# mLSTM cell and leaky-ReLU feed-forward on one core: half of a weight's loads on a second queue, and another hand order for the first chunk

## The chip, the cores and the metric

One NeuronCore of a Trainium2 chip runs the whole program. Its engines work side by side, each through its own list of instructions in order: TensorE (PE; its weight loads are shown as PEld), VectorE (DVE), ScalarE (ACT), GpSimd (POOL) and SyncE (SP). Transfers between the chip's main memory (HBM) and the on-chip memory (SBUF, 128 partitions) are started by an instruction on SP, ACT or POOL and carried by 16 DMA engines. Matmul results go to PSUM.

The metric is the device time of one execution in microseconds (us), the median of several.

## The reference, cut to what matters

```python
# q, k, v, o_gate: (4, 8, 768, 40) float32;  i_gate, f_gate: (4, 8, 768) float32
for t in range(S):                               # mLSTM cell, per batch and head
    m_new  = max(f[t] + m, i[t])
    f_stab = exp(f[t] + m - m_new);  i_stab = exp(i[t] - m_new);  m = m_new
    C = f_stab * C + i_stab * outer(v[t], k[t])  # 40 x 40 state
    n = f_stab * n + i_stab * k[t]
    y[t] = sigmoid(o[t]) * (C @ q[t]) / max(|n . q[t]|, 1)
x = y as (3072 tokens, 320)
h = x @ w_in                                     # 320 x 2048
out = max(0.01 * h, h) @ w_out                   # 2048 x 320
```

The two weights arrive as 64-bit floats (they were scaled by a 64-bit number), so a w_in of 320 x 2048 is 5.24 MB in HBM, as is w_out.

## The kernel before, in words

**Chunks and steps.** The 768 positions are cut into 6 chunks c of 128. A step s = 4c + b is chunk c of batch b, with its 8 heads. `NL = 4` sets of k, q, v and state tiles (`kn`, `qn`, `S0` to `S3`) go round, and `NR = 2` tiles `rb` for the later loads. The feed-forward of chunk c - 1 (`ff_units`, L777) runs on PE between the cell units of chunk c (`cell_units`, L842); chunk 0 has no feed-forward to lie beside it and is written out by hand in `first_chunk` (L887), with the first two feed-forward units `ffs[0]` and `ffs[1]` in it.

**Chunk 0.** `gates(c)` (L289) makes the stabilised gates with two scans and small operations on DVE, into one buffer each; `gates_exp` adds exponentials on ACT; `gates_T` (L341) transposes them through PE and copies them to `gT` on DVE. `spread_mask` and `spread_first` (L442, L453) build the decay matrix in PSUM with PE: a causal mask (`ident_b`, a bf16 identity, times `cmask`) and then the gate rows. `prep_exp` (L474) takes its exponential on ACT into `w`. `u_transpose` (L565) transposes k and q of a step on PE and copies them out (`kqT`), `u_scores` (L576) multiplies them and DVE weights the scores with `w` (L587), `u_values` (L660) multiplies by v and makes the denominators, `gate` (L668) applies the output gate (its second multiply on POOL, or on DVE where that is named), `u_x` (L756) transposes the result into `xT` through five copies, `u_state` (L650) makes the state at the chunk's end from `vu` (`prep_vu`, L483, on POOL) and copies it into the S tiles. `prepare_step` (L160) and `prepare_tiles` (L152) set constants on POOL. The steps 0 to 3 share one set of four PSUM banks for all this (`psc`) and another four for mask and feed-forward (`psf`).

**Chunk 1 and later.** `u_split` (L547) transposes k and q of a step of chunk 1 in halves (line L557), `split_qs` transposes the decayed q (L543), `u_parts` (L621) makes scores and state additions (L637, L642), `u_plain` (L679) the values (L688). `ahead(s)` prepares a step on ACT and POOL, `feed(s)` issues its k, v and decay loads.

**Feed-forward.** The first half of a unit multiplies x by w_in into `ph` (L783), ACT applies the leaky ReLU into `acts` (L791), the parts multiply `acts` by w_out into `po` (L818). w_in is held as two stacks of 64 partitions: the lower half `r = 0` and the upper half `r = 1`, in quarters n of 512 columns. For chunk 0 the units are 16 halves of 20 matmuls, then 16 parts; two of the halves lie in `first_chunk`, so the loop over i (L996) begins with the third, and the parts begin at i = 14.

**Weights.** `load_weights(n)` (L199) loads a raw 64-bit block: n = 0 to 3 are the quarters of w_in, each as four transfers on SP (L227), two for each half of the partitions; n = 4 to 11 are the eight blocks of w_out (L233), issued on ACT's queue at the units i named in `fetch` (L983). A w_out block from the third on lands in a buffer which an earlier block's conversion must have left. `narrow_weights(n)` (L235) turns a raw block into float32, in six instructions of ACT and DVE, as a generator: each `run(w, k)` issues the next k of them. For n < 2 the form is ACT (L248), DVE (L250, L254, L258), ACT (L260), DVE (L262); for the others ACT (L265, L267), DVE (L269), ACT (L273), DVE (L275, L279). In the loop the generator `now` runs through blocks 2 to 11, a few instructions at each i (L998).

**What sets the order.** PE, DVE, ACT and POOL do their work in the order of the code (`manual_schedule`, L971). SP's order is chosen by a scheduler from the code's order and its own estimates. Each transfer takes one of eight completion semaphores in turn, whichever of SP and ACT issues it, and waits for the transfer that had the same one before; so at most eight are under way on these two queues, and a queue can wait for a transfer of the other.

Of the kernel before, what the change touches and what calls it, by code (L numbers as in the profile page):

```python
# [21 lines left out]
def kernel(  # L22
# [81 lines left out]
    zeros = consts.tile([P, 1], F32, name="zeros")  # L104
    nc.vector.memset(zeros[:], 0.0)
    first = consts.tile([P, 1], F32, name="first")
    nc.scalar.activation(first[:], zeros[:], AF.Exp)


    ident_b = consts.tile([P, P], BF16, name="ident_b")  # L110
# [3 lines left out]
        cmask[:], cmask[:], compare_op=ALU.is_ge, fill=-1e30,  # L114
        base=0, pattern=[[1, P]], channel_multiplier=-1,
    )
    nc.vector.tensor_copy(ident_b[:], ident[:])
    cm2 = i0[:, :SL]


# [12 lines left out]
    for n in range(NL):  # L133
        nc.vector.memset(kn[:, n, :, D:], 0.0)
        nc.vector.memset(qn[:, n, :, D:], 0.0)
        nc.gpsimd.memset(S_t[n][:, 1, :, D:], 2.0)
        nc.gpsimd.memset(S_t[n][SL:, 0], 0.0)

    def mixed(s):

# [39 lines left out]
        at = (2 * slot + e) * P  # L180
        return w_in[DP * r : DP * (r + 1), n, at : at + P]

    def run_of(r, at):

        ks = SLOTS[r][at:]
        return ks[0], next((i for i in range(1, len(ks)) if ks[i] != ks[i - 1] + 2), len(ks))

    HW = 2 * Dm
    wide = moe_w_in.dtype == U64
    raws = {}  # L190
# [5 lines left out]
        ks = SLOTS[r][at:]  # L196
        return ks[0], next((i for i in range(1, len(ks)) if ks[i] != ks[i - 1] + 2), len(ks))

    def load_weights(n):  # L199

        m = n - QN
        if n < QN:
            dst = w_in[:, n, :]
        else:
            dst = w_out[:, 2 * m : 2 * m + 2, :].rearrange("p a d -> p (a d)")
        to = dst
        if wide:
            if n < 2:
                at = NF * GT - 2 * WC * (n + 1)
                raw = acts_l[:, at : at + 2 * WC].bitcast(U64)  # L210
            elif n < QN:
                raw = raw_t[:, WC * (n - 2) : WC * (n - 1)]
            elif m < 2:
                raw = w_out[:].rearrange("p f d -> p (f d)")[:, (2 + m) * WC : (3 + m) * WC].bitcast(U64)
            else:
                at = (4, 0, 1, 2, 3, 4)[m - 2] * HW
                raw = raw_t[:, at : at + HW]
            raws[n] = (raw, dst)
            to = raw
        if n < QN:  # L220
            src = moe_w_in[:, n * QC : (n + 1) * QC].rearrange("(k p) (r c) -> r p k c", p=DP, r=2)
            by_slot = to.rearrange("p (k c) -> p k c", k=KC)
            for r in range(2):
                at = 0
                while at < KC:
                    k0, many = run_of(r, at)
                    nc.sync.dma_start(  # L227
                        by_slot[DP * r : DP * (r + 1), at : at + many, :], src[r, :, k0 : k0 + 2 * many - 1 : 2, :],
                    )
                    at += many  # L230
        else:
            rows = moe_w_out[2 * m * P : 2 * (m + 1) * P, :]
            nc.scalar.dma_start(to.rearrange("p (a d) -> p a d", d=Dm), rows.rearrange("(a p) d -> p a d", p=P))  # L233

    def narrow_weights(n):  # L235

        if not wide:
            return  # L240
        raw, dst = raws.pop(n)
        words = raw.bitcast(U32).rearrange("p (c two) -> p c two", two=2)
        lo, hi = words[:, :, 0], words[:, :, 1]
        d = dst.bitcast(U32)
        words = raw.bitcast(U32)[:, : dst.shape[-1]]
        ends = words.bitcast(U16).rearrange("p (c two) -> p c two", two=2)
        if n < 2:
            nc.scalar.activation(dst, hi.bitcast(F32), AF.Abs)  # L248
            yield
            nc.vector.tensor_scalar(  # L250
                dst, dst, scalar1=2.0**-15, scalar2=122879.9921875, op0=ALU.max, op1=ALU.min,
            )
            yield
            nc.vector.tensor_scalar(  # L254
                d, d, scalar1=0x07FFFFFF, scalar2=3, op0=ALU.bitwise_and, op1=ALU.logical_shift_left,
            )
            yield
            nc.vector.scalar_tensor_tensor(d, in0=hi, scalar=0xC0000000, in1=d, op0=ALU.bitwise_and, op1=ALU.bitwise_or)  # L258
            yield
            nc.scalar.activation(words, lo, AF.Copy, scale=2.0**-29)  # L260
            yield
            nc.vector.tensor_tensor(d, d, words, op=ALU.add)  # L262
            yield
            return
        nc.scalar.activation(dst, hi.bitcast(F32), AF.Abs, scale=2.0**16)  # L265
        yield
        nc.scalar.activation(ends[:, :, 0], lo, AF.Copy, scale=2.0**-29)  # L267
        yield
        nc.vector.tensor_scalar(  # L269
            dst, dst, scalar1=2.0, scalar2=122879.9921875 * 2.0**16, op0=ALU.max, op1=ALU.min,  # L270
        )
        yield
        nc.scalar.activation(ends[:, :, 1].bitcast(F16), hi.bitcast(F32), AF.Copy, scale=2.0**-126)  # L273
        yield
        nc.vector.tensor_scalar(  # L275
            d, d, scalar1=0x1FFFFFFF, scalar2=3, op0=ALU.bitwise_and, op1=ALU.logical_shift_left,
        )
        yield
        nc.vector.tensor_tensor(d, d, words, op=ALU.add)  # L279
        yield  # L280
# [100 lines left out]
    def load_o(s):  # L381
        c, b = divmod(s, B)
        at = NF * GT - 4 * WC - (s + 1) * Dm
        st[s]["o"] = acts_l[:, at : at + Dm]
        nc.sync.dma_start(
            st[s]["o"].rearrange("p (h d) -> p h d", d=D), o_gate[b, :, ts(c, P), :].rearrange("h p d -> p h d"),
        )
# [86 lines left out]
    def prep_exp(s):  # L474

        c, b = divmod(s, B)
        w = st[s]["w"]
        for h in range(H):
            bh = b * H + h
            of = st[s]["ab"][h % RG][:, h // RG, :] if c == 0 else w[:, h, :]  # L480
            yield nc.scalar.activation(w[:, h, :], of, AF.Exp, bias=gT[c][:, 0, bh : bh + 1], scale=1.0)  # L481
# [168 lines left out]
    def u_state(s):  # L650
        state(s)
        state_copy(s)
# [186 lines left out]
    def u_gates(c):  # L839
        gates_T(c, bus.pop(c)[0])  # L840
# [15 lines left out]
    def run(steps, n=None):  # L856

        for _ in range(H if n is None else n):
            next(steps, None)
# [27 lines left out]
    def first_chunk():  # L887

        tensor_copy = nc.vector.tensor_copy
        for part in (slice(0, 2), slice(2, 3)):  # L890
            load(0, part)
            load(1, part)
        load_o(0)
        load_o(1)
        load_weights(0)
        load(2)
        load(3)
        load_o(2)
        load_o(3)
        load_weights(1)  # L900
        load_weights(2)
        warm(5)
        spread_mask(0)
        warm(2)
        gates(0)
        gates_exp(0)
        load_fi(2)
        bu, a, _ = bus[0]
        spread_first(a, 0)
        gates_T(0, bu)  # L910
        run(prep_exp(0))
        u_transpose(0, tensor_copy)
        prep_vu(0)
        gates(1)
        u_transpose(1, tensor_copy)
        u_scores(0)
        run(prep_exp(1))
        prepare_tiles()
        prep_vu(1)
        u_scores(1)  # L920
        u_state(0)
        gates_exp(1)
        prep_o(0)
        prep_o(1)
        u_values(0)
        gate(0)
        spread_mask(2)
        spread_first(a, 2)
        run(prep_exp(2))
        u_state(1)  # L930
        u_x(0, tensor_copy)
        u_values(1)
        gate(1, nc.vector)
        w = narrow_weights(0)
        run(w, 3)
        run(prep_exp(3))
        u_gates(1)
        u_x(1)
        prep_vu(2)
        u_transpose(2, tensor_copy)  # L940
        run(w, 2)
        u_scores(2)
        run(w)
        u_transpose(3)
        prep_o(2)
        prep_o(3)
        ffs = ff_units(0)
        ffs[0]()
        prep_vu(3)
        prepare_step(0)  # L950
        prepare_step(1)
        u_values(2)
        gate(2, nc.vector)
        u_scores(3)
        u_x(2)
        ffs[1]()
        u_state(2)
        w = narrow_weights(1)
        run(w, 2)
        u_values(3)  # L960
        gate(3, nc.vector)
        run(w, 2)
        u_x(3)
        u_state(3)
        run(w)
        prepare_step(2)
        prepare_step(3)
        return ffs

    E = mybir.EngineType  # L970
    with tc.manual_schedule(engines={E.PE, E.DVE, E.Activation, E.Pool}):  # L971
        ffs = first_chunk()
        for s in (B, B + 1):
            feed(s)
            for i in range(1, 3):
                load_late(s, i)
        load_weights(3)
        for s in (B + 2, B + 3):
            feed(s)


        ffs = ffs[2:]
        fetch = {4: (0, 1, 2), 6: (3, 4), 10: (5, 6), 15: (7,)}  # L983
        place = (2, 5, 7, 10, 12, 15, 16, 18, 21, 22, 24, 26, 28)
        late = {}
        masks = {0: (2, 3), 12: (4, 5)}
# [2 lines left out]
        for c in range(1, NB + 1):  # L989
# [5 lines left out]
            waiting = []  # L995
            for i in range(n_ff):  # L996
                if c == 1:
                    run(now, (2, 2, 2, 0, 2, 2, 2)[i] if i < 7 else 2 if i < 13 else 3)  # L998
                    for n in fetch.get(i, ()):
                        load_weights(QN + n)  # L1000
                    if i == 0:
                        prep_mask(B)
                        ahead(B)
                        load_fi(3)
# [70 lines left out]
```

## Time and profile before

| | |
|---|---|
| median of 3 runs (lowest to highest) | 544.42 us (544.06 to 544.57) |
| profiled execution | 544.73 us |
| its span, first to last instruction | 542.9 us |
| mean granted PE clock | 0.965 |
| busy: PE, PEld | 520.1 us (96%), 341.3 us (63%) |
| busy: DVE, ACT, POOL | 206.8 us (38%), 184.3 us (34%), 107.3 us (20%) |
| moved by DMA | 59.12 MB, mean 109 GB/s |

Two groups of matmuls hold most of PE's time: `ph` (L783), 1120 of them, 221.0 us, and `po` (L818), 768, 211.1 us. The rest of the profile is read by stretches of time, since the first part of the span differs from all that follows. A row of the time line has start, length, engine, line, operation, tiles and count, and in brackets the idle time before it with what ended that. In the table by stretches an engine's figure is its busy time in that stretch; the clock is the share of full speed that PE was granted; the DMA share is the mean busy share of the 16 DMA engines as recorded, which can exceed 1.

### The profile page before, as it was taken

What the parts mean: (1) busy time and instruction counts of PE and PEld (TensorE: products, weight loads), DVE (VectorE), ACT (ScalarE), POOL (GpSimd) and SP (SyncE); (2) the same over time, 40 slices, a digit from 0 to 9 for tenths busy, and PEclk for the clock granted to TensorE, in tenths of its full rate; (3) what the DMA queues carried; (4) which work ended last, traced back from release to release, by engine and by line L of the source; (5) the groups of instructions that cost most, each with busy time, mean ns of one, the idle gap of its engine ahead of it and who ended that gap; (6) DMA issues with size and microseconds to landing.
All of it is one profiled execution on the core that took longest, in us unless ns stands there. A gap on an engine that the chain in (4) does not pass through costs nothing.

```text
span 542.9 us, 11240 instructions
## 1 busy us (share of the span) xinstructions
PE 520.1 (96%) x4495; PEld 341.3 (63%) x4495; DVE 206.8 (38%) x396; ACT 184.3 (34%) x470; POOL 107.3 (20%) x142
## 2 busy tenths in 40 slices
PE   7877797999999999999999999999999999999997
PEld 6666687977755467755467755567655577644675
DVE  3674632546803826304728124538025521000000
ACT  3363855879652511212503022522013410022100
POOL 4132304323400503102404003303012100000000
PEclk9758798999999999999999999999999999999999
DMA  9998969954623553566642666554651123000000
GB/s 123 157 208 128 167 129 244 227 128 94 139 78 70 124 132 82 146 133 136 149 124 69 146 126 145 147 126 105 147 130 37 38 62 85 24 1 0 13 12 24
DMA packets 164899, 59.12 MB, mean 109 GB/s; under 512 B 128432, under 2 KB 155632, under 8 KB 164848
## 3 DMA queue, kind: packets, MB, share of 16 engines
q1 hardware_dynamic: 162288, 53.04, 47.1%
q10 hardware_dynamic: 2560, 5.37, 3.2%
q8 instruction: 35, 0.57, 0.5%
q14 instruction: 16, 0.13, 0.1%
HBM read 51.68 MB, written 6.70 MB: 108 GB/s over the span
## 4 chain that ended last, share of the span: by engine, by line
PE 87%; DMA 4%; DVE 4%; SPq 2%; ACT 1%; issue 1%; ACTq 0%; DVEq 0%
PE po L818 39%; PE ph L783 37%; PE pT L718 3%; PE sd L637 3%; DMA rb<-in_k_dram 1%; PE pa L664 1%; DMA S<-in_v_dram 1%; PE sd L642 1%; PE ab L460 1%; PE ab L448 1%; DVE kqT L574 1%; PE sc L583 1%; PE hN L688 1%; DMA a_dr<-a 1%; SPq L430 1%
## 5 line engine op out<-in xcount | busy, mean ns | idle before, releaser
L783 PE MATMUL ph<-xT,w_in 64*128 64x512 f32 (+1 forms) x1120 | 221.0, 548 | 7.0 <-ACT acts L791 6.2
L818 PE MATMUL po<-w_out,acts 128*128 128x320 f32 x768 | 211.1, 434 | 0.0
L818 PEld LDWEIGHTS po<-w_out,acts 128*128 128x128 f32 x768 | 144.4, 190 | 62.6 <-issue 3.8
L783 PEld LDWEIGHTS ph<-xT,w_in 64*128 64x128 f32 x1120 | 114.0, 196 | 101.1 <-issue 88.3
L791 ACT ACTIVATE acts<-ph 128x512 f32<-128x512 f32 (+1 forms) x112 | 53.9, 533 | 149.8 <-PE ph L783 146.1
L647 DVE TENSOR_TENSOR qn<-w,sd 64x512 f32<-64x512 f32 x40 | 27.4, 684 | 119.3 <-PE sd L642 64.0
L615 POOL TENSOR_TENSOR S<-S,f 40x336 f32<-40x336 f32 x36 | 29.7, 824 | 136.3 <-PE pT L718 75.5
L472 POOL TENSOR_TENSOR w<-w,i 128x512 f32<-128x512 f32 x20 | 28.0, 1406 | 94.7 <-DMA w<-a_dr 72.6
L481 ACT ACTIVATE w<-w,gT 128x64 f32<-128x64 f32 x160 | 41.3, 338 | 4.7 <-POOL w L472 4.7
L826 ACT COPY y<-po 128x320 f32<-128x320 f32 x12 | 5.1, 425 | 83.7 <-PE po L818 83.7
L826 ACT COPY hn<-po 128x320 f32<-128x320 f32 x12 | 5.1, 426 | 76.9 <-PE po L818 76.9
L534 DVE TENSOR_TENSOR qn<-kqT,ea 64x512 f32<-64x512 f32 x32 | 26.9, 839 | 0.9
L725 DVE STREAM_TRANSPOSE hb<-pT 128x512 f32<-128x512 f32 x16 | 11.4, 715 | 39.1 <-PE pT L718 38.9
L732 POOL TENSOR_TENSOR xb<-xb,den 128x320 f32<-128x320 f32 x16 | 11.6, 727 | 66.6 <-DVE xb L729 66.6
L637 PEld LDWEIGHTS sd<-kqT 40*64 40x64 f32 x640 | 19.9, 135 | 6.1 <-issue 6.1
L637 PE MATMUL sd<-kqT 40*64 40x64 f32 x640 | 21.6, 220 | 0.0
L736 DVE STREAM_TRANSPOSE x<-xb 128x512 f32<-128x512 f32 x16 | 18.1, 1129 | 7.7 <-POOL xb L732 7.7
L528 DVE STREAM_TRANSPOSE kqT<-rb 128x512 f32<-128x512 f32 x32 | 20.5, 679 | 0.0
L642 PE MATMUL sd<-S,vu 64*40 64x42 f32 x576 | 20.0, 214 | 0.4 <-POOL vu L501 0.4
L642 PEld LDWEIGHTS sd<-S,vu 64*40 64x40 f32 x576 | 18.6, 111 | 0.5 <-POOL vu L501 0.5
L619 DVE TENSOR_TENSOR S<-S,sd 40x336 f32<-40x336 f32 x36 | 18.1, 503 | 1.0
L718 PEld LDWEIGHTS pT<-qn,S 128*64 128x64 f32 x512 | 15.6, 138 | 3.6 <-issue 3.5
(135 smaller groups left out, 357.2 us busy)
## 6 DMA issues: line engine op xcount, KB each, us to landing
w<-a_dr SPq DMA_DIRECT2D x40, 128.0 KB
rb<-in_k_dram SPq DMA_DIRECT2D x64, 80.0 KB
rb<-in_q_dram SPq DMA_DIRECT2D x64, 80.0 KB
rb<-in_o_gate_dram SPq DMA_DIRECT2D x64, 80.0 KB
ea<-a_dr SPq DMA_DIRECT2D x32, 128.0 KB
kn<-in_k_dram SPq DMA_DIRECT2D x24, 160.0 KB
raw<-in_moe_w_out_dram ACTq DMA_DIRECT2D x6, 640.0 KB
S<-in_v_dram SPq DMA_DIRECT2D x80, 40.0 KB
```

What stands on the lines that cost most here:

```text
L472: nc.gpsimd.tensor_tensor(w, w, cm2.unsqueeze(1).to_broadcast([P, H, SL]), op=ALU.add)
L481: yield nc.scalar.activation(w[:, h, :], of, AF.Exp, bias=gT[c][:, 0, bh : bh + 1], scale=1.0)
L528: nc.vector.transpose(d["kqT"][:, i].rearrange("p (h t n) -> p h n t", n=TS, t=QW), raw_blocks(s, i, QW).rearrange("p (h n) d -> p h n d", ...
L534: nc.vector.tensor_tensor(mixed(s)[rows, 1 - r], d["kqT"][rows, 1].rearrange("p (h t) -> p h t", t=SL), d["ea"][rows], op=ALU.mult,)
L615: nc.gpsimd.tensor_tensor(new, old, g, op=ALU.mult)
L637: nc.tensor.matmul(bank[1 - u][toks, h, :], lhsT=kqT[rows, 0, ts(h, SL)], rhs=kqT[rows, 1, ts(h, SL)], start=True, stop=True,)
L642: nc.tensor.matmul(dC[u][:, h].rearrange("p k d -> p (k d)"), lhsT=d["ku"][toks, h], rhs=S_v[s % NL][toks, u, h, :, :V1], start=True, stop ...
L647: nc.vector.tensor_tensor(mixed(s)[toks, u], w[toks], bank[1 - u][toks], op=ALU.mult)
L718: nc.tensor.matmul(pT[DP * r : DP * (r + 1), j * P + u * SL : j * P + (u + 1) * SL], lhsT=S[:, u, h, :], rhs=m[:, u, h, :], start=True, st ...
L783: nc.tensor.matmul(ph[r][:, cols], lhsT=w_row(r, slot, j), rhs=xT[DP * r : DP * (r + 1), slot, cols], start=(slot == 0), stop=(slot == KC ...
L791: nc.scalar.activation(acts[:, f, cols], ph[r][:, cols], AF.Prelu, alpha=0.01)
L818: nc.tensor.matmul(po[n][:], lhsT=acts[:, f, ts(n, P)], rhs=w_out[:, f, :], start=(f == 0), stop=(f == NF - 1),)
```

## The change

- `load_weights` gets an argument `halves`. The lower half of a w_in quarter is loaded on SP, the upper half on POOL's own queue. In chunk 0 the two are called in different places; the fourth quarter has both in one call, but each still goes to its queue.
- The eight blocks of w_out are issued on SP instead of ACT: three ahead of the loop, five at the units 4, 8 and 15.
- The second quarter of w_in is converted in the form with three ACT steps (`n < 1` for `n < 2`).
- In chunk 0: the first exponential (which loads ACT's table), the bf16 identity and the setting of the S tiles move into `first_chunk`, behind the first POOL load; on DVE the identity now stands ahead of the first gate scans. `gates(1)` stands before the copies of the transposes. `u_state`, `u_x(0)`, `u_gates(1)`, `prepare_tiles` and the conversions get other places, and `gate(1)`'s second multiply goes from DVE to POOL.
- In the loop the generator `now` issues 2 instructions at each i below 10, 3 below 14 and then 4.
- A function that stood twice is there once, and a `return` stands twice; neither changes what is done.

```diff
-    nc.scalar.activation(first[:], zeros[:], AF.Exp)
-    nc.vector.tensor_copy(ident_b[:], ident[:])
-        nc.gpsimd.memset(S_t[n][:, 1, :, D:], 2.0)
-        nc.gpsimd.memset(S_t[n][SL:, 0], 0.0)
...
-    def load_weights(n):
+    def load_weights(n, halves=(0, 1)):
...
-            for r in range(2):
+            for r in halves:
...
-                    nc.sync.dma_start(
+                    (nc.gpsimd if r else nc.sync).dma_start(
...
-            nc.scalar.dma_start(to.rearrange("p (a d) -> p a d", d=Dm), rows.rearrange("(a p) d -> p a d", p=P))
+            nc.sync.dma_start(to.rearrange("p (a d) -> p a d", d=Dm), rows.rearrange("(a p) d -> p a d", p=P))
...
-        if n < 2:
+        if n < 1:
...
     def first_chunk():
         tensor_copy = nc.vector.tensor_copy
+        load_weights(0, (1,))
+        for n in range(NL):
+            nc.gpsimd.memset(S_t[n][:, 1, :, D:], 2.0)
+            nc.gpsimd.memset(S_t[n][SL:, 0], 0.0)
+        nc.scalar.activation(first[:], zeros[:], AF.Exp)
+        nc.vector.tensor_copy(ident_b[:], ident[:])
         for part in (slice(0, 2), slice(2, 3)):
             load(0, part)
             load(1, part)
+        load_weights(0, (0,))
         load_o(0)
         load_o(1)
-        load_weights(0)
...
-        load_weights(1)
-        load_weights(2)
+        load_weights(1, (0,))
+        load_weights(2, (0,))
...
         gates_T(0, bu)
+        gates(1)
         run(prep_exp(0))
         u_transpose(0, tensor_copy)
         prep_vu(0)
-        gates(1)
         u_transpose(1, tensor_copy)
         u_scores(0)
         run(prep_exp(1))
-        prepare_tiles()
         prep_vu(1)
+        load_weights(1, (1,))
         u_scores(1)
-        u_state(0)
         gates_exp(1)
         prep_o(0)
         prep_o(1)
-        u_values(0)
-        gate(0)
         spread_mask(2)
         spread_first(a, 2)
         run(prep_exp(2))
-        u_state(1)
+        u_values(0)
+        gate(0)
+        w = narrow_weights(0)
+        next(w)
+        u_values(1)
+        run(w, 1)
+        gate(1)
+        run(w, 1)
+        run(prep_exp(3))
         u_x(0, tensor_copy)
-        u_values(1)
-        gate(1, nc.vector)
-        w = narrow_weights(0)
-        run(w, 3)
-        run(prep_exp(3))
-        u_gates(1)
+        load_weights(2, (1,))
+        prepare_step(0)
+        u_transpose(2)
+        run(w, 2)
         u_x(1)
-        prep_vu(2)
-        u_transpose(2, tensor_copy)
-        run(w, 2)
+        u_transpose(3)
+        run(w)
         u_scores(2)
-        run(w)
-        u_transpose(3)
         prep_o(2)
         prep_o(3)
         ffs = ff_units(0)
         ffs[0]()
+        u_state(0)
+        u_state(1)
+        prep_vu(2)
         prep_vu(3)
-        prepare_step(0)
         prepare_step(1)
+        prepare_tiles()
         u_values(2)
         gate(2, nc.vector)
+        w = narrow_weights(1)
+        run(w, 2)
         u_scores(3)
         u_x(2)
         ffs[1]()
-        u_state(2)
-        w = narrow_weights(1)
-        run(w, 2)
+        run(w, 1)
         u_values(3)
         gate(3, nc.vector)
-        run(w, 2)
+        run(w, 1)
+        u_gates(1)
         u_x(3)
+        run(w)
+        u_state(2)
         u_state(3)
-        run(w)
...
-        load_weights(3)
+            if s == B:
+                load_weights(3)
+        for n in range(3):
+            load_weights(QN + n)
...
-        fetch = {4: (0, 1, 2), 6: (3, 4), 10: (5, 6), 15: (7,)}
+        fetch = {4: (3, 4), 8: (5, 6), 15: (7,)}
...
-                    run(now, (2, 2, 2, 0, 2, 2, 2)[i] if i < 7 else 2 if i < 13 else 3)
+                    run(now, 2 if i < 10 else 3 if i < 14 else 4)
```

More of the change, by code (lines that the diff above doesn't have):

```diff
@@ L181, in w_row @@
         return w_in[DP * r : DP * (r + 1), n, at : at + P]
-    def run_of(r, at):
-        ks = SLOTS[r][at:]
-        return ks[0], next((i for i in range(1, len(ks)) if ks[i] != ks[i - 1] + 2), len(ks))
     HW = 2 * Dm
@@ L956, in first_chunk @@
         ffs[1]()
-        u_state(2)
-        w = narrow_weights(1)
-        run(w, 2)
+        run(w, 1)
         u_values(3)
         gate(3, nc.vector)
-        run(w, 2)
+        run(w, 1)
+        u_gates(1)
         u_x(3)
+        run(w)
+        u_state(2)
         u_state(3)
-        run(w)
         prepare_step(2)
         prepare_step(3)
+        return ffs
         return ffs
```

## The prediction

> **What bounds the kernel now.** I read the table by stretches first, to see where TensorE (PE) loses time. Columns: stretch, length, busy time of PE, PEld, DVE, ACT, POOL, granted clock, DMA share, GB/s.
>
> ```profile
> 0.00:14.00 14.00, 10.80 (x84) 8.90 (x84) 5.82 (x21) 5.05 (x16) 6.97 (x24) 1.00 1.04 128
> 14.00:28.00 14.00, 11.72 (x127) 9.81 (x125) 8.64 (x24) 5.52 (x20) 2.05 (x5) 0.76 0.99 155
> 28.00:42.00 14.00, 10.39 (x55) 8.68 (x56) 9.19 (x16) 7.39 (x19) 4.26 (x9) 0.51 1.10 207
> ...
> 57.00:76.00 19.00, 16.41 (x234) 13.93 (x228) 9.36 (x17) 14.87 (x32) 2.46 (x2) 0.86 0.87 135
> 76.00:93.00 17.00, 13.54 (x258) 12.14 (x254) 5.22 (x8) 8.85 (x15) 6.59 (x6) 0.90 0.93 213
> 93.00:135.00 42.00, 41.28 (x570) 33.56 (x571) 22.43 (x42) 35.58 (x76) 13.30 (x14) 0.96 0.68 157
> 135.00:158.00 23.00, 23.00 (x123) 15.80 (x123) 12.13 (x24) 14.49 (x44) 7.62 (x7) 1.00 0.54 133
> ```
>
> From 93 us on PE is busy nearly all the time at clock 0.96 to 1.00: whatever is gained before that is kept, and nothing can be gained after it. Before 93 us PE idles (3.6 us of 14 in 28 to 42) and runs at half clock after its idle times. The change works only there.
>
> Next the chain of waits, to see who holds PE in chunk 0 (start, length, what):
>
> ```profile
> 26.24 0.42 DVE xT L768
> ...
> 30.09 0.84 DVE w_in L250
> ...
> 30.96 1.11 DVE w_in L254
> ...
> 33.70 2.10 PE sc L583 x16
> ...
> 37.07 1.41 DVE w_in L262
> ...
> 38.53 4.11 PE ph L783 x20
> ```
>
> DVE alone carries it from 25.5 to 33.6 us and again to 38.5: its order of work, not data, holds back the first feed-forward matmuls. Last the time line of ACT in the loop:
>
> ```profile
> 77.13 1.21 ACTq L233 DMA_DIRECT2D w_out<-in_moe_w_out_dram  x2
> 81.72 0.37 ACTq L233 DMA_DIRECT2D raw<-in_moe_w_out_dram  x1
> 82.14 0.66 ACT L791 ACTIVATE acts<-ph 128x256 f32<-128x256 f32 x2 [3.38 <-DMA w_out<-in_moe_w_out_dram]
> ...
> 90.42 1.69 ACTq L233 DMA_DIRECT2D raw<-in_moe_w_out_dram  x2
> 92.23 0.82 ACT L481 ACTIVATE w<-w,gT 128x64 f32<-128x64 f32 x3 [4.67 <-POOL w L472]
> ```
>
> ACT stands 3.38 us in front of its own w_out issue, and again 4.67 us (named for POOL's L472, but the L233 issues stand directly before the activation). PE's next ph matmuls wait for its relu L791: 1.87 us before 82.58, 1.73 us before 93.52, both followed by clock 0.50.
>
> **The change, part by part** (lines of before; clock times are mine where no row is named).
>
> *ident_b first on DVE.* PE's mask matmuls L448 waited 1.66 us for it, behind the gate scans. The warm-ups end at 1.47 + 2.50 = 3.97, so all up to the gT copy moves from 10.58 to 8.9: minus 1.66. The gate chain pays 0.20 us, inside DVE's 1.56 us wait for f.
>
> *gates(1) before the kqT copies.* It ran 12.72 to 15.05 between two pairs of copies. Now: 8.9 + 0.23 (gT) + 2.33 (gates) + 4 x 0.64 (copies) = 14.0, when scores(1) can start; it was 16.30. Minus 2.3.
>
> *State, transposes and u_gates moved back.* After scores(1): 1.16 to 15.2, mask and spread 3.93 (21.06 to 24.99) to 19.1, two u_values. One took 3.43 at half clock (17.83), one 1.88 at full (25.74): they end at 23.0 or 26.0, against 27.62. I take 23.0: the idle time before them (11.1 to 12.8) is shorter than the 2.28 us that preceded the drop in before. Two u_state (0.51 each), one u_x (0.53) and u_gates (0.82) are paid later.
>
> *First quarter's conversion.* On DVE after values(1): denominators 0.6, L250 0.84, x 0.46, L254 1.11, xT(0) copies 1.88, L258 1.48, then ACT L260 1.37, DVE L262 1.49: 23.0 + 9.2 = 32.2; it was 38.48. The second scores wait for xT(1)'s copies (1.65 on ACT behind L260), so ffs[0] starts at about 34.2, not 38.53: minus 4.3.
>
> *To the first split of chunk 1 (L557).* ffs[0] 4.11 (half clock) to 38.3, two states 1.0, values(2) 1.98, denominators and x(2) 1.7 (scores(3) inside), u_x 0.67, ffs[1] 2.43, values(3) 1.98, x(3) 1.7 (u_gates now inside, where PE stood 3.05 us before 54.57), u_x 0.67, states 1.0: 51.4. The second bank waits for ACT's xT(3) copies: 52.0 against 56.09, **minus 4.1**. Ends: 50.7 with ffs[0] at full clock, 54.9 with both early values at half. The second quarter's shorter conversion has three ACT steps (1.39, 1.65, 1.63, rows L265, L267, L273) for two of 1.37, and loses DVE's L258 (1.94): it lies under ffs[1] and values(3); without that cover it would cost about 2 us.
>
> *w_out issued by SP.* L557 to the first po took 113.56 - 56.09 = 57.5 us. ACT's work in it, in the new order: 14 relu pairs at 0.6 = 8.4; two quarters at 4.65 = 9.3; three w_out blocks at 2.64 and two steps of a fourth 9.6; kqT copies 3 x 2.36, exps 3 x 2.2, tq copies 3 x 1.18, tanhs 0.9, gate exps 1.0: 46.4. PE's: 14 x 2.36 = 33.0, L557, L543, L637/L642, L688 12.5: 45.5. Taking away ACT's stalls, 3.38 + 4.67, and one late L260 (1.36, 57.75) gives 48.1, just above both. As the two engines are then equally full I add 0.9: 49.0, **minus 8.5**. On SP the three first w_out now stand ahead of v and w of s = 6 and 7, needed some 40 us later, which hides 3 x 0.66 MB at 309 GB/s = 6.4 us; the later five wait on SP for conversions (ACT and DVE), with loads of c = 2 behind them, needed after the first po. Where that cover goes, each us of it is a us on s = 6.
>
> *k of s = 4 and 5.* State(0) now follows ffs[0], so SP issues k(4), k(5) behind v and w of both, two q, two o, and the third prepare_step on POOL: I put k(4)'s landing between 48 and 55, PE wants it at 52. Cost 0 to 3; I take 1.0.
>
> *Upper halves of w_in on POOL.* No row shows a POOL issue. Bounds for one: 0.32 us (SP's L415 at 86.71) to 5.53 (SP's L371 at 15.05); nearest is the same transfer from SP, 2.74/4 = 0.69, which I take. POOL's idle times, 5.87 before L491 and 7.93 before L677, hide pairs of that; above some 4 us each they would not. What it does to the transfers: w_in, 64 partitions at a time, moves 207 GB/s in 28 to 42 with the engines full, while w_out, all 128, moves more:
>
> ```profile
> 81.00:87.00 6.00, 4.42 (x24) 4.42 (x26) 1.73 (x3) 4.79 (x10) 1.16 (x2) 0.72 1.09 309
> ```
>
> So a half quarter (0.66 MB) is 3.2 us at 207 and 2.1 at 309. Bounds: four upper halves wholly beside other loads, 12.8 us of transfer gone; or nothing gone, and the first one delays k and q of s = 0, 1 by up to 3.2. Neither is on my path, DVE being it until 34 us; it sets only k(4)'s bounds above. I count 0.
>
> Here the Trainium skill speaks against the change: "SBUF — State Buffer", section "Can I just issue two DMAs to hit both halves?", says two transfers to the two partition halves serialize (only 6% over one), and only one transfer over all 128 partitions reaches all ports. The rows agree that 64 partitions move less; no row shows two halves at once. By the page nothing of the 12.8 us goes and k(4) lands at the late end, 2 us more than my sum.
>
> *Order on SP.* w0's lower half passes o(0), o(1): their tanhs (15.72) move to about 18.5, hidden by exp(2), which waits for spread_first until 19.1. Without that, 1 us per us.
>
> **Sum.** The profiled execution took 544.73 (span 542.9 and 1.8 around it): 544.73 - 4.1 - 8.5 + 1.0 = 533.1. The runs' median is 0.31 lower, so 532.8, rounded **533**.
>
> **Rivals.**
> 1. *Only chunk 0 pays* (22%). Against the loop gain: ACT and PE leave no slack (46.4 and 45.5 in 49), and SP now carries all loads with DMA share about 0.9 already. Loop gain 1.5 instead of 8.5: 540.
> 2. *POOL's queue becomes the bound* (13%). For it: no row prices its issue, and two go ahead of gate(0)'s multiply, two ahead of prep_mask(4). Slack: 13.5 to 22.2 for the first, about 48 to 55.5 less 1.3 for the second. At d us per issue the cost is 2d - 8.7 and 2d - 6.2; from d = 6.5 the gain of 11.6 is eaten; at 8 us, past SP's worst row, it costs 17.1: 550. Against: POOL is 20% busy.
> 3. *The loads bound everything before 93 us* (3%). DMA share 0.87 to 1.10 for it; the DVE chain and ACT's stalls against. Then the reordering moves nothing: 544.4.
>
> **How the numbers follow.** Forecast 62%. Its own range: early end 50.7 (minus 5.4), the loop at ACT's floor of 46.4 (minus 11.1) and k(4) in time give 528; late end 54.9 (minus 1.2) and k(4) 3 us late give 538. Rival 1 spreads over 537 to 543, and PE's floor of 45.5 with half the relus hidden would add 1 to 2 us of gain: **526 to 543** leaves out rivals 2 and 3 and a little of rest. About 0.2% is what a measurement here can tell. Faster by more: 62 + 21 = 83%; within 0.2%: 3 + 1 = 4%; slower: 13%.
>
> **What would show it.** Right: gT copy near 9 us, the first quarter's last step done at 32 to 33, the first split near 53, no issue on ACT's queue after the gates, first po near 102, no half clock after 60. Wrong: POOL issues above 4 us, PE or ACT waiting for k(4), DVE still on the chain to 38 us, or new idle time of PE after 93 us while SP waits for a conversion.

## The result, and the profile after

| | before | after |
|---|---|---|
| median (lowest to highest), side by side, 5 runs each | 544.25 us (544.04 to 544.57) | 539.91 us (538.47 to 541.74) |
| profiled execution, its span | 544.73, 542.9 us | 539.92, 537.9 us |
| mean granted PE clock | 0.965 | 0.962 |
| busy PE, DVE, ACT, POOL | 520.1, 206.8, 184.3, 107.3 us | 515.5, 204.5, 187.6, 111.5 us |

Ratio 0.992, 95% interval 0.9897 to 0.9943: faster by 4.3 us (0.8%), where 11.6 were forecast. In the changed kernel most line numbers after the first hundred are 9 lower: the split of chunk 1 is L548, `ph` L774, `po` L809, k's load L364, the w_out loads L224.

The table by stretches of the changed kernel, columns as before:

```profile
14.00:28.00 14.00, 13.55 (x111) 10.97 (x107) 6.59 (x17) 8.40 (x27) 4.88 (x8) 0.62 1.16 170
28.00:42.00 14.00, 12.05 (x89) 9.10 (x88) 6.50 (x11) 6.24 (x13) 3.31 (x9) 0.55 1.14 182
...
57.00:76.00 19.00, 12.14 (x224) 10.58 (x226) 4.04 (x11) 8.89 (x22) 1.95 (x2) 0.71 1.02 202
76.00:93.00 17.00, 17.00 (x310) 15.54 (x310) 7.78 (x12) 15.56 (x34) 4.89 (x6) 1.00 0.73 169
93.00:135.00 42.00, 42.00 (x602) 32.65 (x599) 31.31 (x55) 33.49 (x70) 15.81 (x17) 1.00 0.79 160
```

From 76 to 135 us PE has no idle time at all and full clock (before: 13.54 of 17 at 0.90): what the loop lost is gone. But 57 to 76 got worse, 12.14 us of 19 at 0.71 instead of 16.41 at 0.86. The chain of waits of that stretch (start, length, what) names the cause:

```profile
52.37 1.14 SPq L421
...
53.57 0.94 SPq L421
...
54.56 0.58 SPq L390
...
55.18 0.98 SPq L390
...
56.26 7.47 DMA kn<-in_k_dram
...
63.86 2.06 PE tk L548 x64
```

The chain has left the computing engines. It runs along SP's list of issues (L421 the decays `w` of s = 5, L390 its q and o) to the load of k for s = 4, issued at 56.26 and landed 7.47 us later. The row of PE, with the idle time and its cause in brackets, and SP's time line before it:

```profile
63.86 0.42 PE L548 MATMUL tk<-ident,kn 64*40 64x64 f32 x3 [10.37 <-DMA kn<-in_k_dram]
```

```profile
36.24 5.55 SPq L367 DMA_DIRECT2D S<-in_v_dram  x4
44.96 1.12 SPq L421 DMA_DIRECT2D w<-a_dr  x2
...
47.38 1.77 SPq L218 DMA_DIRECT2D raw<-in_moe_w_in_dram  x2
49.20 2.68 SPq L367 DMA_DIRECT2D S<-in_v_dram  x4
51.97 2.53 SPq L421 DMA_DIRECT2D w<-a_dr  x2
...
56.26 4.87 SPq L364 DMA_DIRECT2D kn<-in_k_dram  x2
```

k(4)'s tile was free when state(0) ended, at about 40.7 (an estimate: the two states run from 40.15 to 41.16 on PE). Its load stood behind v, w, q and o of s = 4 and 5 and half of the fourth quarter of w_in. In the kernel before, state(0) ran at 17.4 and k(4) was issued at 34.06, ahead of all of these:

```profile
17.39 0.51 PE L595 MATMUL dC<-vu,kn 128*40 128x42 f32 x16
...
34.06 0.37 SPq L373 DMA_DIRECT2D kn<-in_k_dram  x1
```

The start of the first split and of the first `po` before, and of the first `po` after:

```profile
56.09 0.33 PE L557 MATMUL tk<-ident,kn 64*40 64x64 f32 x2
...
113.49 4.57 PE L818 MATMUL po<-w_out,acts 128*128 128x320 f32 x16
```

```profile
108.45 4.58 PE L809 MATMUL po<-w_out,acts 128*128 128x320 f32 x16
```

So the time divides as follows: the split could have begun at 53.9 (its last xT copy ends then) instead of 56.09, **minus 2.2**; it waited to 63.86, **plus 10.0**; from there to the first `po` it took 44.6 us (108.45) instead of 57.4 (113.49), **minus 12.8**. Together minus 5.0, which is the difference of the spans.

### The profile page after: what moved, and what is told of

It is laid out like the page before. It is cut to its first block, busy times and chain, and to the rows that moved or that the text cites. A ratio compares the mean times of both kernels' runs of the same rounds, so it can differ in the third digit from the quotient of the medians.

```text
span 537.9 us, 11254 instructions
## 1 busy us (share of the span) xinstructions
PE 515.5 (96%) x4495; PEld 335.5 (62%) x4495; DVE 204.5 (38%) x392; ACT 187.6 (35%) x473; POOL 111.5 (21%) x151
## 4 chain that ended last, share of the span: by engine, by line
PE 88%; DMA 1%; SPq 1%; DVE 0%; ACT 0%; issue 0%; ACTq 0%
PE po L809 39%; PE ph L774 39%; PE pT L709 3%; PE sd L628 3%; DMA kn<-in_k_dram 1%; PE tk L548 1%; PE sd L633 1%; PE hN L679 1%; PE tq L534 1%; SPq L421 0%; PE tg L341 0%; SPq L390 0%; PE tg L336 0%; DVE w_in L266 0%; PE xt L756 0%; PE xt L757 0%
## 5 line engine op out<-in xcount | busy, mean ns | idle before, releaser
L774 PE MATMUL ph<-xT,w_in 64*128 64x512 f32 (+1 forms) x1120 | 216.5, 539 | 0.0
L809 PE MATMUL po<-w_out,acts 128*128 128x320 f32 x768 | 211.1, 434 | 0.0
L809 PEld LDWEIGHTS po<-w_out,acts 128*128 128x128 f32 x768 | 144.5, 190 | 62.6 <-issue 3.8
L774 PEld LDWEIGHTS ph<-xT,w_in 64*128 64x128 f32 x1120 | 109.4, 191 | 93.4 <-issue 88.3
L782 ACT ACTIVATE acts<-ph 128x512 f32<-128x512 f32 (+1 forms) x112 | 53.9, 532 | 141.5 <-PE ph L774 141.3
L606 POOL TENSOR_TENSOR S<-S,f 40x336 f32<-40x336 f32 x36 | 28.5, 792 | 131.5 <-PE pT L709 75.4
L472 ACT ACTIVATE w<-w,gT 128x64 f32<-128x64 f32 x160 | 41.2, 338 | 0.0
```

The lines of the kernel that those rows point to most:

```text
L606: nc.gpsimd.tensor_tensor(new, old, g, op=ALU.mult)
L774: nc.tensor.matmul(ph[r][:, cols], lhsT=w_row(r, slot, j), rhs=xT[DP * r : DP * (r + 1), slot, cols], start=(slot == 0), stop=(slot == KC ...
L782: nc.scalar.activation(acts[:, f, cols], ph[r][:, cols], AF.Prelu, alpha=0.01)
L809: nc.tensor.matmul(po[n][:], lhsT=acts[:, f, ts(n, P)], rhs=w_out[:, f, :], start=(f == 0), stop=(f == NF - 1),)
```

## The experiments

Theory: the 10 us come from k(4)'s *place on SP's queue*. Rivals: the stream of loads is full before 64 us, so that whatever goes first something else is late; or the transfers that POOL issues hold the others up. In kernels with k moved, lines after the new function are 8 higher (the split is L556).

**k(4) and k(5) on POOL's queue.**

```diff
         u_state(0)
         u_state(1)
+        load_k(B)          # nc.gpsimd.dma_start; load(s) then leaves k out
+        load_k(B + 1)
```

> k of s = 4 and 5 are issued from GpSimd's queue right after the two states that free their tiles; all else as in the changed kernel (539.9 us). Place theory: the 10.4 us in front of the first split come from the place of k(4) on SyncE's queue (issued at 56.26, though free from 41.2). Then k(4) is issued near 41.5 and lands by 47, PE finds it there, the split begins at 53.5 to 55 instead of 63.9; the loop to the first po takes 47 to 49 instead of 45.1, because the two steps of the third quarter that ScalarE did during the wait (3.0 us) come back into it; the time is 531 to 534. Rival, a full load stream: whatever comes first, some other load of s = 4 or 5 (v, w, q) is then late by nearly as much, the first split or the cell after it waits 7 us or more for a DMA, and the time stays above 537. Rival, GpSimd's transfers are slow beside SyncE's: k(4) lands after 53 and half or less of the wait goes: 535 to 538.

Measured: 529.63 us, ratio to before 0.9729 (0.971 to 0.9749), a little below the expected 531 to 534. POOL's and PE's rows:

```profile
40.27 1.79 POOL L378 DMA_DIRECT2D kn<-in_k_dram  x2 [9.97 <-PE dC L594]
```

```profile
53.01 0.33 PE L556 MATMUL tk<-ident,kn 64*40 64x64 f32 x1 [0.79 <-ACT xT L771]
...
98.52 4.57 PE L817 MATMUL po<-w_out,acts 128*128 128x320 f32 x16
```

The same loads, issued 16 us earlier (40.27 instead of 56.26), and PE's wait for k is gone: they landed 6.5 us after their issue. Two matmuls of the split run at 51.92; the rest begins at 53.01, after 0.79 us for ACT's copies, the wait that the prediction had put there. From there on PE is busy without a gap up to the first `po`: no other load took the place of k. Full stream and slow POOL transfers both fall. The loop takes 45.5 us from 53.0: ACT's two steps of the third quarter (1.37 and 1.64 us), which ran inside the wait, cost less than 1 us of the 3.0 when they come back.

**The states early again, SP's list as it then falls.** `u_state(0)` goes back behind `u_scores(1)`, `u_state(1)` behind `spread_first(a, 2)`; nothing else.

> The changed kernel with the states of s = 0 and 1 back at their old places before the early values (one after scores(1), one after the mask of s = 2), so that k(4) and k(5) are free at about 20 us and stand early on SyncE's queue again. Place theory: the wait of 10.4 us in front of the first split goes; the two states cost PE 1 us at full clock or 2 at half ahead of the values, so the first split begins at 54.5 to 57; with the loop at 47 to 49 the time is 532 to 535. Full load stream: k(4) early pushes v, w and q of s = 4 back by the same, a wait for one of these takes its place and the time stays above 537.

Measured: 528.87 us, 0.9705 (0.9684 to 0.9727), below the expected 532 to 535. The scheduler puts k(4) ahead of v(4) again:

```profile
36.81 0.37 SPq L364 DMA_DIRECT2D kn<-in_k_dram  x1
```

```profile
49.49 0.30 PE L548 MATMUL tk<-ident,kn 64*40 64x64 f32 x2
```

The split begins at 49.5, its second bank at 50.6, 4 to 6 us earlier than expected: in this kernel the states cost nothing ahead of the values. A new wait does appear later, behind the first `po`: 2.3 us of PE at 103.6, for q of s = 7. Two different edits that share only k's issue time remove the 10 us: the place on the queue is the cause.

**The first upper half later.**

```diff
-        load_weights(0, (1,))
         for n in range(NL):
             nc.gpsimd.memset(S_t[n][:, 1, :, D:], 2.0)
...
         gates(1)
+        load_weights(0, (1,))
         run(prep_exp(0))
```

> The changed kernel with the first upper half (of quarter 0) issued from GpSimd only after its memsets (about 6.6 us instead of 1.65), behind the gates' loads of 32 partitions. Place theory: the gate scan that waited 4.38 us for its load starts near 4.5 instead of 7.02 and chunk 0 runs 1 to 2.5 us earlier, but the first split still waits for k(4), whose place on SyncE's queue stays late: little of it arrives at the end, 538.5 to 540.5. Rival, GpSimd's transfers are what delays everything, k(4) too: the time falls by the whole 2.4 us, to 537 or less.

> Both edits: k(4) and k(5) from GpSimd's queue after the states, and the first upper half after GpSimd's memsets. Place theory: with k(4) in time nothing else holds the first split, so what chunk 0 gains from the gates' earlier loads (1 to 2.5 us) now reaches the end: 1 to 2.5 us below the kernel with k(4) and k(5) alone moved, 529 to 532. If a full load stream holds the split, this is no faster than that kernel within 0.5 us.

Measured: alone, as expected, 540.2 us, 0.992 (0.9901 to 0.9939), which cannot be told from the changed kernel; with k moved 531.27 us, 0.9764 (0.9746 to 0.9781), no faster than with k alone. The first gate scan of the changed kernel, and of the one with this edit alone:

```profile
7.02 0.42 DVE L287 TENSOR_TENSOR_SCAN F<-f,zeros 128x128 f32<-128x128 f32 x1 [4.38 <-DMA fi<-in_f_gate_dram]
```

```profile
4.04 0.42 DVE L287 TENSOR_TENSOR_SCAN F<-f,zeros 128x128 f32<-128x128 f32 x1 [1.40 <-DMA f<-in_f_gate_dram]
```

So the half quarter that POOL issues at 1.65 us does hold the gates' 16 KB loads back, by 3.0 us, and this gain was lost again further on, even with k in time: my expectation of the second kernel failed. ACT's row in it says where:

```profile
21.61 0.47 ACT L516 ACTIVATE acts<-acts 128x320 f32<-128x320 f32 x1 [8.65 <-DMA acts<-in_o_gate_dram]
```

ACT stands 8.65 us before the first tanh (the output gate's), for o(0), which is issued behind the lower half of quarter 0; the exponentials of s = 2 and the conversion queue up behind it.

**o(0), o(1) ahead of that lower half** (in the last kernel):

```diff
-        load_weights(0, (0,))
         load_o(0)
         load_o(1)
+        load_weights(0, (0,))
```

> The kernel with k(4), k(5) moved and the first upper half issued late (531.3 us), in which ScalarE waited 8.65 us for o(0) behind the lower half of quarter 0; here o(0) and o(1) are issued before that lower half. If o(0) is what ate the gates' gain, the first tanh starts at 17.5 or before instead of 21.6, the first split begins 1.5 to 4 us earlier than at 53.7, and the time is 527 to 530. If the load stream as a whole is full, the half quarter or k(2) is then late instead: the first split stays after 53 and the time above 530.

Measured: 527.97 us, 0.9712 (0.9673 to 0.9751); the first tanh at 16.07, the split at 50.0 (53.7 without this edit). The time and the place are as expected. The next thing late is a load again:

```profile
25.66 1.09 PE L570 MATMUL tkq<-ident,kn 128*128 128x128 f32 x4 [6.28 <-DMA kn<-in_k_dram]
```

**All of w_in on SP** (with k moved): both halves in each call, `nc.sync` for all.

> The kernel with k(4) and k(5) on GpSimd's queue (529.6 us), but all halves of w_in issued by SyncE, each upper half right behind its lower one. If the second queue moves nothing faster (the same bytes in the same time), only the order changes: the gates land early again (scan near 4.1 instead of 6.64), the loads of o and of s = 2 and 3 stand behind one more half of quarter 0; the first split begins within 1.5 us of 51.9 and the time is 528.5 to 531.5. If two queues side by side move more than one, the loads come 3 to 12 us later all through the first 60 us, PE waits for them, and the time is 533 to 541.

Measured: 530.07 us, 0.9744 (0.9709 to 0.978), against 0.9729: the same, as expected if the second queue moves nothing faster. The first 57 us in one row each, with the upper halves on POOL's queue and with all on SP's:

```profile
0.00:57.00 57.00, 43.80 (x445) 35.99 (x447) 31.62 (x77) 32.23 (x75) 28.45 (x57) 0.78 1.09 164
```

```profile
0.00:57.00 57.00, 43.37 (x449) 36.04 (x451) 32.09 (x78) 31.07 (x74) 23.04 (x49) 0.82 1.10 167
```

164 GB/s with two queues, 167 with one, DMA share 1.09 and 1.10. The second queue moved nothing that the first would not have moved. The part of the change which its name puts first is worth nothing that can be measured here. This was tried with k moved only.

**w_out back on ACT** (with k moved):

```diff
-            nc.sync.dma_start(to.rearrange("p (a d) -> p a d", d=Dm), ...
+            nc.scalar.dma_start(to.rearrange("p (a d) -> p a d", d=Dm), ...
```

> The kernel with k(4) and k(5) on GpSimd's queue (529.6 us), but all w_out loads back on ScalarE's queue, at the same places of the program. If ScalarE's waits in front of these issues are the loop's gain, ScalarE stands before its later issues again (before: 3.38 and 4.67 us), PE's idle time comes back, and split to first po is 50 to 56 instead of 46.6: 533 to 539. If the new order of the conversions and of the blocks is what gains, the loop stays below 48.5 and the time below 532.

Measured: 554.13 us, 1.0181 (1.0142 to 1.022): 24.5 us more than with SP, far beyond what was expected. ACT's time line and PE's row after it:

```profile
53.31 0.26 ACT L771 COPY xT<-xt 64x128 f32<-64x128 f32 x1
68.41 1.71 ACTq L224 DMA_DIRECT2D w_out<-in_moe_w_out_dram  x2
76.13 0.43 ACTq L224 DMA_DIRECT2D raw<-in_moe_w_out_dram  x1
76.74 1.35 ACT L256 ACTIVATE w_in<-raw 128x1280 f32<-128x1280 f32 x1 [23.17 <-DMA S<-in_v_dram]
```

```profile
83.32 4.44 PE L782 MATMUL ph<-xT,w_in 64*128 64x256 f32 x20 [21.11 <-ACT acts L790]
```

The three transfers go into memory that is free. What the issues wait for stands in this kernel's list of instructions (each `DMAHW` is one of the eight completion semaphores):

```
L224 DMACopy w_out<-in_moe_w_out_dram 128x2x320 [waits DMAHW4_49]
L224 DMACopy w_out<-in_moe_w_out_dram 128x2x320 [waits DMAHW7_49]
L224 DMACopy raw<-in_moe_w_out_dram 128x2x320 [waits DMAHW2_49]
```

Only completion semaphores, that is, the transfers which had them before; the trace names a load of v (`S<-in_v_dram`) as the last one, which has nothing to do with w_out. ACT, with the relus, kqT copies and conversions behind it in order, stood still until SP's loads had landed, and PE stood 21.11 us for a relu. Here the issues stand ahead of the loop, behind SP's loads of v for s = 7; inside the loop of the kernel before they cost 7.3 us (next experiment), so the size depends on their place. In the kernel before, the issues in front of the 3.38 and the 4.67 us wait for such semaphores too, one of them for a conversion as well.

**Before, with w_out on SP and nothing else:**

> The kernel before (544.3 us) with nothing changed but that SyncE issues the w_out loads instead of ScalarE. The prediction's term alone: split to first po falls from 57.5 by 8.5, up to the 12.4 measured in the changed kernel: 532 to 536. If SyncE now stands before the issues that wait for a conversion and the loads of c = 2 behind them come late, the gain is half or less: 540 or more.

Measured: 536.5 us, 0.9857 (0.9824 to 0.9891), 7.3 us less, just above the expected 532 to 536.

```profile
54.28 0.33 PE L557 MATMUL tk<-ident,kn 64*40 64x64 f32 x2
...
104.58 4.57 PE L818 MATMUL po<-w_out,acts 128*128 128x320 f32 x16
```

Split to first `po` is 50.3 us instead of 57.4, minus 7.1. (The split itself began 1.8 us earlier than before, ahead of any load of w_out; no run says why.) One line moved between two queues is worth more than the whole change was.

**Further down the same road.** The upper halves of quarters 1 and 2 issued later; then also the states early; or also ten warm-up matmuls before `u_transpose(2)`; then all of these.

> The kernel with o(0), o(1) issued first (528.0 us), in which PE waited 6.28 us for k(2) at 25.66, with GpSimd's second and third upper halves issued one place later (quarter 1 near 28 us instead of 16.5, quarter 2 behind k(4), k(5)). If these halves take the stream from SyncE's loads of s = 2, k(2) lands 2 to 3 us earlier, the second scores and the first feed-forward unit follow, and the first split begins at 47.5 to 49.5 instead of 50.0: 525.5 to 527.5. Rival: the upper half of quarter 1 is then late itself (ScalarE waits over 2 us for it near 41) and the time stays at 527.5 to 530.

> The same, and the states of s = 0 and 1 ahead of the early values, so that they run beside DVE's and ScalarE's work there and k(4), k(5) can be issued near 30. The 0.81 us of the two states leave the late part, and cost up to 1 us ahead of the values, where PE waits for loads afterwards anyway (6.28 us before tkq(2)): the first split begins 0.5 to 1.5 us earlier than in the kernel with quarter 1 late, the time falls by as much. If k(4), k(5), now issued before v(4) and w(4), push other loads back, the time is the same or up to 1.5 us longer.

> The kernel with quarter 1's upper half late, and ten more warm-up matmuls (2.5 us at full clock) where PE waits for k(2). If PE's half clock from 20 to 36 us (granted clock 0.50 after the idle time) holds the path there, the clock stays near 1.0, the first feed-forward unit takes 2.5 us instead of 3.55 and the scores and transposes half: 1 to 2 us off the time. If that part hangs on loads, DVE and ScalarE, it gains less than 0.7.

> All edits together: k(4), k(5) on GpSimd's queue, its upper halves later, o(0), o(1) first, the states of s = 0 and 1 ahead of the early values, ten warm-up matmuls before tkq(2). The single ones of the last three gave 527.8, 528.3 and 527.6 us, which cannot be told apart. If what is left of chunk 0 hangs on the conversion of quarter 0 (its lower half lands near 22.7 us, ScalarE and DVE then need 11 us to the first feed-forward unit), the sum is no better than its parts: 526.5 to 528.5. If PE's clock and the states each had a gain that something hid in the single runs, 524.5 to 526.

| kernel | median | ratio to before, interval |
|---|---|---|
| quarters 1, 2 late | 527.78 us | 0.9698 (0.9682 to 0.9714) |
| and states early | 528.25 us | 0.9727 (0.9687 to 0.9767) |
| or warm-ups | 527.56 us | 0.9692 (0.9675 to 0.971) |
| all | 527.92 us | 0.9693 (0.9666 to 0.9719) |

These four cannot be told apart, nor from the kernel with o first. In the first, k(2) did come earlier (23.15 instead of 25.66), but the first feed-forward unit began at 33.87 instead of 34.08, so the time did not follow. With the warm-ups PE's clock from 14 to 28 us was 1.00 instead of 0.74, and that too bought less than 0.7 us, because PE then waited longer for the copies behind the conversion of quarter 0:

```profile
32.05 1.86 PE L582 MATMUL sc<-kqT 40*128 40x128 f32 x13 [3.45 <-ACT xT L771]
```

What is left of chunk 0 seems to hang on quarter 0: its lower half lands at about 22.5, and ACT and DVE then need some 11 us. No run moved that half alone, so this is read from rows and not shown.

With all edits together the warm-ups did not do what they did alone. PE first stood 2.99 us for POOL's `vu` in front of the early state, its clock fell to 0.50 behind that and was 0.52 from 14 to 28 us, and the warm-ups came later and ran slowly. The three rows of that kernel, and the warm-ups of the kernel with them alone:

```profile
15.35 0.79 PE L594 MATMUL dC<-vu,kn 128*40 128x42 f32 x16 [2.99 <-POOL vu L494]
...
20.63 7.05 PE L663 MATMUL pa<-S,w 128*128 128x41 f32 x32
...
28.15 4.07 PE L330 MATMUL warm<-ident 128*128 128x128 f32 x20
```

```profile
19.89 2.40 PE L330 MATMUL warm<-ident 128*128 128x128 f32 x20
```

The time is the same in spite of this, which again suggests that PE does not hold this part. The best versions, at 0.969 to 0.971, beat both kernels: 16 us below the one before, 12 below the changed one.

## Why the prediction was right and wrong

| step of the prediction | forecast | measured |
|---|---|---|
| identity first: gT copy | 8.9 | 9.51; 8.25 with the first upper half late |
| `gates(1)` before the copies: kqT copied | 14.0 | 14.27 |
| two early values end | 23.0 (bound 26.0) | 25.05; 20.99 with k moved |
| first quarter converted | 32.2 | 33.8 |
| `ffs[0]` starts, ends | 34.2, 38.3 | 35.33, 40.2; starts 35.19 with k moved |
| first split could begin | 52.0 (50.7 to 54.9) | 53.9; 53.0 with k moved |
| k of s = 4 and 5 | plus 1.0 (0 to 3) | plus 10.0 |
| split to first po | 49.0 | 44.6; 45.5 with k moved |
| w_out on SP | minus 8.5 | minus 7.1, alone |
| one POOL issue | 0.69 (0.32 to 5.53) | 0.63 to 0.70 |
| upper halves beside other loads | 0 | 0 in the time; the first delays the gate scan by 3.0 |
| w0 ahead of o(0), o(1) | hidden | not hidden |

The forecast chose the right case and the right direction, and the size was off. **The step that failed is "k of s = 4 and 5 ... Cost 0 to 3; I take 1.0".** It had the order on SP right and named what stands ahead of the load, but for half of the fourth quarter of w_in. What it got wrong is when that list gets done: the issue was at 56.26 and the landing at 63.73, not between 48 and 55, a figure for which it gave no working. SP was busy with v(4) to 41.8 and then stood 3.1 us, to 44.96, for the gates' round trip through main memory; the fourteen issues then ahead of k(4) took 11.3 us, and the transfer itself 7.5. The cost was 10.0 us. The two experiments on k's place show the cause; without that term the forecast's median is 531.8, and with k in time 529.63 was measured. The prediction had "PE ... waiting for k(4)" among its signs of being wrong, and that is what was seen.

Three terms were off and partly cancelled: k by plus 9.0, chunk 0 by plus 1.9, the loop by minus 4.4. That 539.9 lies inside the stated 526 to 543 is therefore luck.

*The loop.* "W_out issued by SP" was right in mechanism and near in size: minus 7.1 alone. The loop gained 12.8, and 11.9 with k in time; the other 4.8 come with the rest of the change's order (conversions spread differently over the loop, w_out blocks called at other units), which no run took apart, so this stays argued. With k moved PE has no idle time in the loop's 45.5 us, so PE is what bounds it there. The two floors of the prediction were sums of rows and not exact: ACT was busy for only 41.2 of these 45.5 us, where its sum was 46.4, and the changed kernel's 44.6 lies below PE's sum of 45.5. The 0.9 us added for two full engines was not needed.

*Chunk 0.* Minus 2.2 where 4.1 were forecast. All its steps are there, each late by 0.3 to 2 us. The values look like the reason and are not. They ended 2 us late because the scores ahead of them ran at half clock (3.79 us for both, clock 0.50 from 14 to 17 us; 2.06 with k moved). The 4.41 us of the values themselves are nearly full clock: two took 3.77 at full clock and 7.05 at half. And their lateness cost nothing. The changed kernel, then the one with k moved:

```profile
13.47 3.79 PE L574 MATMUL sc<-kqT 40*128 40x128 f32 x32
...
20.64 4.41 PE L655 MATMUL pa<-S,w 128*128 128x41 f32 x32
```

```profile
17.22 3.77 PE L663 MATMUL pa<-S,w 128*128 128x41 f32 x32
...
25.91 1.09 PE L570 MATMUL tkq<-ident,kn 128*128 128x128 f32 x4 [4.29 <-DMA kn<-in_k_dram]
```

With k moved the values end at 20.99, 4 us earlier, and `ffs[0]` starts at 35.19 instead of 35.33. PE waits 4.29 us for k(2) instead, and ACT waits for o. "Order on SP ... hidden" is the step that failed here: exp(2) stands on ACT behind the tanh of o(1), and the conversion of quarter 0 behind exp(2). With k moved the spread of s = 2 was done at 17.3 and exp(2) began at 21.97, behind that tanh, where the forecast had 19.1 (in the changed kernel 20.7 and 21.18). "Its order of work, not data" was true of the kernel before; once the order is better, data hold it. Putting o first, with the first upper half late, gave 0.5% (0.9712 against 0.9764, intervals that just touch) and the split at 50.0. The first upper half in front of the gates' loads (3.0 us on the scan), which I had priced against k and q only, delays the first steps, but issuing it later did not by itself bring the split forward (53.7 with k moved, against 51.9).

*Rivals.* "Only chunk 0 pays" has nearly the time that was measured (540) and is wrong: the loop paid more than forecast and k took it back. A right number is no proof of its mechanism. POOL's queue did not become a bound: eight issues of 0.63 to 0.70 us. The loads did not bound everything, but after k was moved they were next.

*The skill.* The Trainium skill's page "SBUF — State Buffer", section "Can I just issue two DMAs to hit both halves?", which I weighed against the change, agrees with the runs as far as they go: no gain from two queues (164 and 167 GB/s). No run loads a quarter as one transfer over all 128 partitions. The page "DMA: Bandwidth & Descriptors", section "Issuing engines are not separate DMA queues", adds that starting transfers from several engines saves only the sequencer's time to start them. For bandwidth the runs agree. For the time of a kernel that is not the whole account: which engine issues w_out changed it by 7.3 us in one order and by 24.5 in another, through what waited behind the issue.

## What to carry to other kernels

When a piece of work moves later, look up which load its end sets free and where that load stands on its queue, and time it with the queue's own waits and the landing, not only by the issues ahead. Keep loads off the queues of engines that have work waiting behind them: an issue can wait for somebody else's transfer, and everything behind it waits too. (POOL stood 9.97 us before its issue of k at no cost that shows.) Splitting this load over two queues did not move it faster, but a second queue was a way past a full first one for the one small load that was urgent; an earlier place on the first queue did as well (528.87 us against 529.63). And before working on a late step, look for a run in which it came early: here the values came 4 us earlier and nothing followed.

## What the runs showed of the hardware

- Two transfers of together 0.66 MB, issued at 1.65 us from POOL, held 16 KB loads that ACT and SP issued from 0.75 us on back by 3.0 us (2.4 with k moved: scan at 6.64 and 4.23): small transfers on another queue did not overtake.
- k(4), 160 KB, took 7.47 us from issue to landing with the DMA engines full (share 1.13 in that time); POOL's own transfers took 5.7 to 8.6 us at the median.
- An issue on POOL's queue costs POOL 0.63 to 0.70 us, about what the same transfer cost SP (0.69); with k moved, two issues of k took 1.79.
- With 2.4 us of unneeded matmuls in PE's wait for k(2) its granted clock was 1.00 from 14 to 28 us, where the same kernel without them had 0.74. In the kernel with all edits, which has them too, PE had stood 2.99 us before, its clock from 16 to 28 us was 0.50, and the same matmuls took 4.07 us. This is one execution each.
